# Routing of the first two chunks of a fused attention and expert kernel: small operands in a PSUM bank, comparisons over even then odd columns

## The chip, the cores and the metric

The program runs on one core of a Trainium2 chip. The metric is the device time of one execution in microseconds (us). Of the core's engines, TensorE (PE in the profile) multiplies matrices, VectorE (DVE) and ScalarE (ACT) work element by element on SBUF and PSUM, GpSimd (POOL) works on SBUF alone, and SyncE (SP) issues DMAs. PEld is PE's weight load. Each engine runs its own instructions in order and waits for the others by semaphores.

## What is computed

An attention with clusters as mask feeds a dense layer pair (MoE1), whose output is routed to one of eight experts for each token (MoE2). 2 x 768 = 1536 tokens of 512 values pass through all of it. The change touches the middle of the last function: norm, logits, arg-max, gate.

```python
def _moe_ref(x, w_in, w_out, s, b):            # MoE1: 512 -> 2048 -> 512
    h = x @ w_in
    r = np.maximum(h, 0.0)
    return (s * (r * r) + b) @ w_out

def _moe2_ref(x, expert_emb, tau, w1, w2):     # MoE2: 8 experts, 512 -> 1024 -> 512
    xn = x / (np.linalg.norm(x, axis=-1, keepdims=True) + 1e-06)
    en = expert_emb / (np.linalg.norm(expert_emb, axis=-1, keepdims=True) + 1e-06)
    logits = xn @ en.T / tau
    expert_idx = np.argmax(logits, axis=1)
    logits_shift = logits - logits.max(-1, keepdims=True)
    probs = np.exp(logits_shift)
    probs /= probs.sum(-1, keepdims=True) + 1e-09
    gate_w = probs[np.arange(N), expert_idx]
    for e in range(E):
        mask = expert_idx == e
        out[mask] = gate_w[mask, None] * (np.maximum(x[mask] @ w1[e], 0.0) @ w2[e])
```

## The kernel before

**Stages.** The span has three stages: attention (to about 290 us), MoE1 (to about 588 us), and the experts of MoE2. MoE1 takes the 1536 tokens in three chunks of 512. For a chunk it runs through 16 blocks f of the hidden width: `up(f)` multiplies the chunk by a weight block, `down(f-1)` multiplies the block before by its second weights into four PSUM banks y0 to y3. fp32 products are made from a high and a low part each, three matmuls for one. Per block that is 12 matmuls of up (L552, tile hp) and 12 of down (L560, tile y), each of 512 columns; such a block is called a round here.

**Who feeds a round.** ACT copies the weights' high part (L529, wh), POOL subtracts it for the low part (L531, two 128x512 `tensor_tensor` per round on SBUF). ACT and DVE then turn hp into the inputs of down: L607 (ACT, t), L608 (DVE, hp), L611 (ACT, gh), L612 (DVE, gl). In the last chunk POOL also makes the low part of three weight blocks of the first expert (L545, tile wu) and issues gathers by index (L824).

**Routing beside it.** When a chunk is done, `route` for it is a generator, and MoE1 takes one step of it per round of the next chunk (`next(stages)` in `moe1`), ordered behind that round's L611 and L612. So the routing of the first chunk (c = 0) runs in the rounds of the second, that of the second (c = 1) in the rounds of the third, and that of the third (`final`) after MoE1. Step by step: transposes (tp), projection (lt), logits (lg), arg-max as a one-hot (oh), rank of each token within its expert (rk, rank), `locate` (L721: DVE compares a row of 384 column numbers, `iotas`, with each token's rank, giving the 0/1 matrices ohr, in pieces of 256 and 128 columns), `collect` (L727: PE multiplies ohr with small values into tile si, and DVE adds si into `info`), then the norm by `root` (ACT, L82) and `norm_recip` (DVE, L86 to L91, on tile nr), the shifted logits (L760 to L762, on l), exp (ACT, L766), the gate (L767 to L775, on m, gt, gb, v) and a last `collect` of it. After the second locate, c = 1 also runs `pick` (which expert is worked early) and at its end `take`.

**Order and banks.** Within MoE1 the tile framework's scheduler orders each engine's instructions; there is no table. PSUM has eight banks, named here by tags: "a" stands for the bank pv, "b" for sm; y0 to y3 and M0, M1 (hp, in turns) are the other six. A tile on a tag waits until the last reader of the tile before it on that tag is done.

**The weight conversion.** During the first chunk DVE also turns w_in and w_out from 64-bit to 32-bit floats (`conv_steps`). Its clamp, L425, works in place in SBUF over even, then odd elements; the steps behind it write or read tile cv in PSUM (L430, L435, L437):

```python
s = t.rearrange("p a (w o) -> p o (a w)", o=2)
nc.vector.tensor_scalar(out=s.bitcast(F32), in0=s.bitcast(F32), scalar1=CLAMP_LO, scalar2=CLAMP_HI, op0=ALU.max, op1=ALU.min)
...
nc.vector.scalar_tensor_tensor(out=u[a], in0=r[a][:, :, 1], scalar=0xC0000000, in1=u[a], op0=ALU.bitwise_and, op1=ALU.bitwise_or)
nc.vector.scalar_tensor_tensor(out=t[:, a], in0=r[a][:, :, 0], scalar=29, in1=u[a], op0=ALU.logical_shift_right, op1=ALU.bitwise_or)
```

Of the kernel before, what the change touches and what calls it, by code (L numbers as in the profile page):

```python
# [9 lines left out]
F32 = mybir.dt.float32  # L10
# [6 lines left out]
ALU = mybir.AluOpType  # L17
AX = mybir.AxisListType
# [3 lines left out]
P = 128  # L22
# [17 lines left out]
E, F2 = 8, 1024  # L40
# [40 lines left out]
def root(nc, g):  # L81
    nc.scalar.activation(out=g(1), in_=g(0), func=AF.Sqrt)  # L82


def norm_recip(nc, g):
    nc.vector.tensor_scalar(out=g(4), in0=g(1), scalar1=1e-30, scalar2=None, op0=ALU.max)  # L86
    nc.vector.reciprocal(out=g(5), in_=g(4))
    nc.vector.tensor_tensor(out=g(6), in0=g(0), in1=g(5), op=ALU.mult)
    nc.vector.tensor_tensor(out=g(1), in0=g(6), in1=g(1), op=ALU.add)
    nc.vector.tensor_scalar(out=g(2), in0=g(1), scalar1=0.5, scalar2=1e-6, op0=ALU.mult, op1=ALU.add)  # L90
    nc.vector.reciprocal(out=g(3), in_=g(2))  # L91
# [289 lines left out]
class Moe:  # L381
# [262 lines left out]
    def route(self, c, ys, final):  # L644
        nc = self.nc
        n = len(ys)
        g0 = c * n
        fill = lambda i: final and self.fill(FILL[i])
        rp = self.sm
        bc = lambda a: a.to_broadcast([P, n, E])  # L650
# [10 lines left out]
        yt = []  # L661
        part = rp.tile([P, n, P], F32, name="part", tag="part", bufs=1)

        nr = rp.tile([P, n, 8], F32, name="nr", tag="nr")

        def square(i):
            sq = self.gp.tile([P, DM], F32, name="sq", tag="t", bufs=4)
# [17 lines left out]
        for i, t in enumerate(lt):  # L685
            copy(i, part[:, i * each:(i + 1) * each], t)
        yield
        lg = self.ps([P, n, E], "lg", "M0" if final else "b")
        for i in range(n):
            nc.tensor.matmul(lg[:, i], part[:, i], self.fold)  # L690
        fill(0)
        l = rp.tile([P, n, E], F32, name="l", tag="l")
        w = rp.tile([P, n, E], F32, name="w", tag="w")
        m = rp.tile([P, n, 4], F32, name="m", tag="m")
# [22 lines left out]
        ohr = [rp.tile([P, 3 * P], BF16, name="ohr", tag="ohr", bufs=4) for _ in range(n)]  # L717

        def locate(j0, j1):
            for i in range(n):  # L720
                nc.vector.tensor_scalar(out=ohr[i][:, j0 * P:j1 * P], in0=self.iotas[:, j0 * P:j1 * P], scalar1=self.rank[:, g0 + i:g0 + i + 1], scalar2=None, op0=ALU.is_equal)  # L721

        def collect(j0, j1, v0, v1, tag):
            si = self.ps([P, j1 - j0, v1 - v0, E], "si", tag)
            for j in range(j0, j1):
                for i in range(n):
                    nc.tensor.matmul(si[:, j - j0], ohr[i][:, j * P:(j + 1) * P], v[:, i, v0:v1], start=i == 0, stop=i == n - 1)  # L727
            self.accumulate(self.info[:, j0:j1, v0:v1], si, c)
            if final and v0 == 0:
                if j0 == 0:  # L730
                    self.where = [self.sm.tile([P, 3, E], dt, name=nm, tag=nm, bufs=1) for nm, dt in (("idx", U32), ("off", U32), ("gate", F32), ("dec", F32))]
                self.index(self.where[0][:, j0:j1], self.info[:, j0:j1])

        locate(0, 2)
        yield
        collect(0, 2, 0, 2, "b")
        fill(2)
        yield
        locate(2, 3)
        collect(2, 3, 0, 2, "a")  # L740
        fill(3)
# [14 lines left out]
            yield  # L756
        if not final:
            root(nc, lambda i: nr[:, :, i])
        norm_recip(nc, lambda i: nr[:, :, i])
        nc.vector.tensor_tensor(out=l, in0=l, in1=bc(nr[:, :, 3:4]), op=ALU.mult)  # L760
        nc.vector.tensor_reduce(out=m[:, :, 2:3], in_=l, axis=AX.X, op=ALU.max)
        nc.vector.tensor_tensor(out=l, in0=l, in1=bc(m[:, :, 2:3]), op=ALU.subtract)  # L762
        if final:
            fill(5)
        yield
        nc.scalar.activation(out=l, in_=l, func=AF.Exp)  # L766
        nc.vector.tensor_reduce(out=m[:, :, 3:4], in_=l, axis=AX.X, op=ALU.add)  # L767
        nc.vector.tensor_scalar(out=m[:, :, 3:4], in0=m[:, :, 3:4], scalar1=1e-9, scalar2=None, op0=ALU.add)
        gt = rp.tile([P, n, 4], F32, name="gt", tag="gt")
        gb = rp.tile([P, n, 3], BF16, name="gb", tag="gb")  # L770
        nc.vector.reciprocal(out=gt[:, :, 0:1], in_=m[:, :, 3:4])
        for z in range(3):
# [1 line left out]
            nc.vector.tensor_tensor(out=gt[:, :, z + 1:z + 2], in0=gt[:, :, z:z + 1], in1=gb[:, :, z:z + 1], op=ALU.subtract)  # L774
            nc.vector.tensor_tensor(out=v[:, :, 2 + z], in0=oh, in1=bc(gb[:, :, z:z + 1]), op=ALU.mult)  # L775
        yield
        collect(0, 3, 2, 5, "y0" if final else "b")
        if c == NT // TC - 2:
            self.take()
            yield  # L780
# [3 lines left out]
        if final:  # L784
            _, off, gate, a = self.where
            self.decode(off, gate, a, self.info, self.slot, self.ntok.rearrange("p (o e) -> p o e", o=1).to_broadcast([P, 3, E]))

    def pick(self):
        nc, sm = self.nc, self.sm
        ps = self.ps([P, E], "pk", "b")  # L790
        nc.tensor.matmul(ps, self.ones, self.cum)
        n, w, m0, m, keep, s = [sm.tile([P, E], F32, name=nm, tag=nm, bufs=1) for nm in ("pn", "pw", "pm0", "pm", "pk", "ps")]
        self.m0, self.m, self.keep, self.late, self.drop = m0, m, keep, s[:, 2:3], s[:, 3:4]
        nc.vector.tensor_copy(n, ps)
        nc.vector.tensor_reduce(out=s[:, 0:1], in_=n, axis=AX.X, op=ALU.max)
        nc.vector.scalar_tensor_tensor(out=w, in0=n, scalar=s[:, 0:1], in1=self.desc, op0=ALU.is_equal, op1=ALU.mult)
        nc.vector.tensor_reduce(out=s[:, 1:2], in_=w, axis=AX.X, op=ALU.max)
        nc.vector.tensor_scalar(out=m0, in0=w, scalar1=s[:, 1:2], scalar2=None, op0=ALU.is_equal)
        nc.vector.tensor_scalar(out=s[:, 2:3], in0=s[:, 0:1], scalar1=3.0 * P, scalar2=None, op0=ALU.is_ge)
        nc.vector.tensor_scalar(out=s[:, 3:4], in0=s[:, 0:1], scalar1=float(P), scalar2=None, op0=ALU.is_lt)  # L800
        nc.vector.tensor_scalar(out=s[:, 4:5], in0=s[:, 1:2], scalar1=-1.0, scalar2=float(E), op0=ALU.mult, op1=ALU.add)
        nc.vector.scalar_tensor_tensor(out=s[:, 5:6], in0=s[:, 0:1], scalar=float(P), in1=s[:, 2:3], op0=ALU.is_ge, op1=ALU.subtract)
        nc.vector.tensor_scalar(out=m, in0=m0, scalar1=s[:, 5:6], scalar2=None, op0=ALU.mult)
        nc.vector.tensor_scalar(out=keep, in0=m0, scalar1=s[:, 2:3], scalar2=None, op0=ALU.mult)
        nc.vector.tensor_scalar(out=keep, in0=keep, scalar1=float(2 * P - NT), scalar2=float(NT), op0=ALU.mult, op1=ALU.add)
        up = [self.xp.tile([P, 2, F2], F32, name="eup", tag=f"xt{i}") for i in range(2)]
        down = [self.xp.tile([P, 4, DM], F32, name="edn", tag="xt2")] + [self.raw.tile([P, 2, DM], F32, name="edn", tag="raw") for _ in range(2)]
        self.eup = [up[k // 2][:, k % 2] for k in range(KD)]
        self.edown = [down[0][:, f] if f < 4 else down[f // 2 - 1][:, f % 2] for f in range(NF2)]
        self.eload = []  # L810
        for tiles, src, each in ((up, self.w1, KD), (down, self.w2, NF2)):
            r0 = 0
            for i, t in enumerate(tiles):
                n = t.shape[1]
                r = sm.tile([P, 1], U32, name="wr", tag=f"wr{each}{i}", bufs=1)
                nc.vector.scalar_tensor_tensor(out=r, in0=s[:, 4:5], scalar=float(P), in1=self.iotap, op0=ALU.mult, op1=ALU.add)
                nc.vector.tensor_scalar(out=r, in0=r, scalar1=float(each // n), scalar2=float(r0 // n), op0=ALU.mult, op1=ALU.add)
                self.eload.append((t, src.rearrange("e (q r) w -> (e q) (r w)", r=n), r))
                r0 += n
# [34 lines left out]
    def fill(self, n):  # L854
        for _ in range(n):
            next(self.early, None)
# [335 lines left out]
```

## Time and profile before

| What | Value |
| --- | --- |
| Median of 3 runs | 823.32 us (821.75 to 825.11) |
| Profiled execution, its own time | 824.21 us |
| Its span in the profile | 822.3 us |
| PE busy | 769.7 us (94%) |
| DVE busy | 526.9 us (64%) |
| ACT busy | 421.6 us (51%) |
| POOL busy | 347.5 us (42%) |

The engines' busy times are sums over the whole span. Times in the rows are counted from the span's start. In a row of the timeline the first number is the start, the second how long the row lasted, from the start of its first instruction to the end of its last; a bracket at the end holds the idle time of the engine before it and who ended it. An instruction that is held up inside its engine is not idle there: it shows as a long one.

### The profile page before, as it was taken

What the parts mean: (1) busy time and instruction counts of PE and PEld (TensorE: products, weight loads), DVE (VectorE), ACT (ScalarE), POOL (GpSimd) and SP (SyncE); (2) the same over time, 40 slices, a digit from 0 to 9 for tenths busy, and PEclk for the clock granted to TensorE, in tenths of its full rate; (3) what the DMA queues carried; (4) which work ended last, traced back from release to release, by engine and by line L of the source; (5) the groups of instructions that cost most, each with busy time, mean ns of one, the idle gap of its engine ahead of it and who ended that gap; (6) DMA issues with size and microseconds to landing.
All of it is one profiled execution on the core that took longest, in us unless ns stands there. A gap on an engine that the chain in (4) does not pass through costs nothing. (4 is left out here: it accounts for less than half of the span.)

```text
span 822.3 us, 12229 instructions
## 1 busy us (share of the span) xinstructions
PE 769.7 (94%) x4191; PEld 580.2 (71%) x4193; DVE 526.9 (64%) x1087; ACT 421.6 (51%) x841; POOL 347.5 (42%) x277
## 2 busy tenths in 40 slices
PE   7699999898998889999999999997999999999994
PEld 3456555454554458888778787775879998989883
DVE  5769789695895779994353642648446635756650
ACT  5355465454653665646445554444346645756651
POOL 2067766575674655435434443445032202220000
PEclk9799999998998999999999999989999999999998
DMA  5155423334232205611000042254131844876600
GB/s 147 49 139 175 124 72 92 111 91 119 73 76 63 60 22 170 184 55 52 1 1 1 7 147 86 94 191 142 65 103 58 272 141 157 236 259 228 211 17 23
DMA packets 75470, 88.73 MB, mean 108 GB/s; under 512 B 7445, under 2 KB 58549, under 8 KB 75008
## 3 DMA queue, kind: packets, MB, share of 16 engines
q1 hardware_dynamic: 68704, 69.67, 27.9%
q0 software_dynamic: 4000, 13.90, 5.3%
q10 hardware_dynamic: 2688, 4.19, 1.7%
q8 instruction: 40, 0.66, 0.3%
q14 instruction: 38, 0.31, 0.1%
HBM read 70.57 MB, written 7.34 MB: 95 GB/s over the span
## 5 line engine op out<-in xcount | busy, mean ns | idle before, releaser
L531 POOL TENSOR_TENSOR wl<-w,wh 128x512 fp32r<-128x512 f32 x96 | 123.1, 1307 | 131.5 <-ACT wh L529 128.9
L249 ACT ACTIVATE pt<-S 128x384 f32<-128x384 f32 x192 | 91.6, 490 | 123.1 <-PE S L248 121.0
L224 DVE TENSOR_REDUCE mx<-M 128x1 f32<-128x384 f32 x192 | 101.8, 551 | 54.8 <-PE M L223 52.8
L260 POOL TENSOR_TENSOR acc<-acc,pt 128x768 f32<-128x768 f32 x61 | 106.1, 1740 | 6.5 <-ACT pt L249 4.1
L552 PE MATMUL hp<-x,wh 128*128 128x512 f32 x384 | 107.2, 400 | 0.3 <-ACT wh L529 0.3
L552 PE MATMUL hp<-x,spare 128*128 128x256 f32 x732 | 96.1, 284 | 2.0 <-PEq L984 1.7
L552 PEld LDWEIGHTS hp<-x,spare 128*128 128x128 f32 x732 | 92.7, 190 | 6.9 <-issue 4.1
L560 PE MATMUL y<-wd,gg 128*128 128x512 f32 x360 | 93.2, 395 | 0.0
L608 DVE SCALAR_TENSOR_TENSOR hp<-hp,sb,t 128x512 f32<-128x512 f32 x48 | 36.3, 757 | 78.8 <-ACT t L607 78.8
L247 PE MATMUL S<-qa,ka 97*128 97x384 f32 x192 | 72.5, 377 | 13.2 <-DMA qa<-mrs 11.5
L552 PEld LDWEIGHTS hp<-x,wh 128*128 128x128 f32 x384 | 71.9, 191 | 15.5 <-ACT wh L529 0.9
L223 PE MATMUL M<-ka,qa 80*128 80x384 f32 x192 | 79.0, 412 | 3.6 <-DVE mx L224 2.3
L268 PE MATMUL pv<-pt,vn 128*64 128x385 f32 x384 | 78.8, 534 | 0.0
L560 PE MATMUL y<-wh,gh 128*128 128x512 f32 x192 | 75.6, 394 | 1.7 <-ACT gh L611 1.7
L560 PE MATMUL y<-wl,gh 128*128 128x512 f32 x192 | 75.3, 392 | 0.0
L545 DVE TENSOR_TENSOR wd<-w,wd 128x512 fp32r<-128x512 f32 x64 | 43.3, 686 | 44.4 <-ACT wd L544 41.0
L560 PEld LDWEIGHTS y<-wd,gg 128*128 128x128 f32 x360 | 63.7, 189 | 10.1 <-DVE gg L1081 0.2
L1033 POOL DMA_INDIRECT row<-rows,idx x24 | 28.0, 1166 | 95.7 <-PE tp L1045 50.8
L248 PE MATMUL S<-qb,kb 128*128 128x384 f32 x192 | 66.7, 347 | 0.0
L607 ACT ACTIVATE t<-hp 128x512 f32<-128x512 f32 x48 | 28.7, 598 | 73.9 <-PE hp L552 73.9
L223 PEld LDWEIGHTS M<-ka,qa 80*128 80x128 f32 x192 | 37.1, 193 | 39.2 <-issue 8.2
L560 PE MATMUL y<-wh,gl 128*128 128x512 f32 x192 | 59.4, 391 | 0.0
(269 smaller groups left out, 1371.8 us busy)
## 6 DMA issues: line engine op xcount, KB each, us to landing
w<-in_moe_w_dram SPq DMA_DIRECT2D x128, 256.0 KB
raw<-in_moe_w_in_dram SPq DMA_DIRECT2D x12, 512.0 KB
raw<-in_moe_w_out_dram SPq DMA_DIRECT2D x12, 512.0 KB
qn<-in_q_dram SPq DMA_DIRECT2D x16, 192.0 KB
kn<-in_k_dram SPq DMA_DIRECT2D x16, 192.0 KB
vn<-in_v_dram SPq DMA_DIRECT2D x16, 192.0 KB
ka<-kb SPq DMA_DIRECT2D x16, 192.0 KB
qa<-qb SPq DMA_DIRECT2D x16, 192.0 KB
```

Of the source, the lines that this page charges most:

```text
L223: nc.tensor.matmul(pp, qa[i][0:80, r * P:(r + 1) * P], ka[i][0:80, c * HS:(c + 1) * HS])
L224: nc.vector.tensor_reduce(out=mxt[j % 2][:, r, c:c + 1], in_=pp, axis=AX.X, op=ALU.max)
L247: nc.tensor.matmul(pp, ka[i][0:97, t * P:(t + 1) * P], qa[i][0:97, w], start=True, stop=False)
L248: nc.tensor.matmul(pp, kb[i][:, t * P:(t + 1) * P], qb[i][:, w], start=False, stop=True)
L249: exps.setdefault((j, t), []).append(nc.scalar.activation(out=p[:, c, 0:HS], in_=pp, func=AF.Exp, scale=0.125).ins)
L260: eng.tensor_tensor(out=acc[j][-1], in0=acc[j][-1], in1=p[:, :, 0:HS], op=ALU.add)
L268: together(tc, [lambda c=c: nc.tensor.matmul(pv_t[j][c * 64:c * 64 + 64, :], io_t["v", j][:, t, :], p[:, c, :], start=t == 0, stop=t == NR ...
L531: eng.tensor_tensor(out=wl[:, a], in0=w[:, a], in1=wh[:, a].bitcast(F32), op=ALU.subtract)
L545: eng.tensor_tensor(out=t[:, 1], in0=w[:, a], in1=t[:, 0].bitcast(F32), op=ALU.subtract)
L552: self.nc.tensor.matmul(hp, a[:, k * P:(k + 1) * P], b(k), start=n == 0, stop=n == 3 * KD - 1)
L560: self.nc.tensor.matmul(y[i], (gl if n == 2 else gh)[:, s], wl if n == 1 else wh, start=first and n == 0, stop=last and n == 2)
L608: nc.vector.scalar_tensor_tensor(out=hp, in0=hp, scalar=sb[:, 0:1], in1=t, op0=ALU.mult, op1=ALU.mult)
```

## The change

In the routing of all three chunks one PSUM tile `rt` takes the place of `lg`, on the same tag ("b", in the final chunk M0), and lives until the gate is done. It holds the logits (`lg`), the intermediate results of `norm_recip` and the row maximum (`nb`, eight numbers per token tile) and the gate's residues (`gt`), which were SBUF tiles; of `nr` two columns stay in SBUF, the squared norm and its root. In the first two chunks the tiles `si` and `pk`, which were on "b", go to "a", and `locate` compares the even columns first and then the odd ones, in one instruction with a pattern of 2 x 128 (or 2 x 64) in steps of two.

```diff
-        nr = rp.tile([P, n, 8], F32, name="nr", tag="nr")
+        nr = rp.tile([P, n, 2], F32, name="nr", tag="nr")
...
-        lg = self.ps([P, n, E], "lg", "M0" if final else "b")
+        rt = self.ps([P, 3, n, 32], "rt", "M0" if final else "b")
+        lg, nb, gt = rt[:, 0, :, 0:E], rt[:, 1, :, 0:8], rt[:, 2, :, 0:4]
...
         def locate(j0, j1):
             for i in range(n):
-                nc.vector.tensor_scalar(out=ohr[i][:, j0 * P:j1 * P], in0=self.iotas[:, j0 * P:j1 * P], scalar1=self.rank[:, g0 + i:g0 + i + 1], scalar2=None, op0=ALU.is_equal)
+                o, s = [t[:, j0 * P:j1 * P] for t in (ohr[i], self.iotas)]
+                if not final:
+                    o, s = [t.rearrange("p (w o) -> p o w", o=2) for t in (o, s)]
+                nc.vector.tensor_scalar(out=o, in0=s, scalar1=self.rank[:, g0 + i:g0 + i + 1], scalar2=None, op0=ALU.is_equal)
...
-        collect(0, 2, 0, 2, "b")
+        collect(0, 2, 0, 2, "b" if final else "a")
...
-        norm_recip(nc, lambda i: nr[:, :, i])
-        nc.vector.tensor_tensor(out=l, in0=l, in1=bc(nr[:, :, 3:4]), op=ALU.mult)
-        nc.vector.tensor_reduce(out=m[:, :, 2:3], in_=l, axis=AX.X, op=ALU.max)
-        nc.vector.tensor_tensor(out=l, in0=l, in1=bc(m[:, :, 2:3]), op=ALU.subtract)
+        norm_recip(nc, lambda i: (nr if i < 2 else nb)[:, :, i])
+        nc.vector.tensor_tensor(out=l, in0=l, in1=bc(nb[:, :, 3:4]), op=ALU.mult)
+        nc.vector.tensor_reduce(out=nb[:, :, 7:8], in_=l, axis=AX.X, op=ALU.max)
+        nc.vector.tensor_tensor(out=l, in0=l, in1=bc(nb[:, :, 7:8]), op=ALU.subtract)
...
-        gt = rp.tile([P, n, 4], F32, name="gt", tag="gt")
...
-        collect(0, 3, 2, 5, "y0" if final else "b")
+        collect(0, 3, 2, 5, "y0" if final else "a")
...
-        ps = self.ps([P, E], "pk", "b")
+        ps = self.ps([P, E], "pk", "a")
```

DVE's norm step in the routing of the second chunk, before:

```order
L86 TENSOR_SCALAR nr<-nr 128x4
L87 RECIPROCAL nr<-nr 128x4
L88 TENSOR_TENSOR nr<-nr 128x4
L89 TENSOR_TENSOR nr<-nr 128x4
L90 TENSOR_SCALAR nr<-nr 128x4
L91 RECIPROCAL nr<-nr 128x4
L760 TENSOR_TENSOR l<-l,nr 128x32
L761 TENSOR_REDUCE m<-l 128x4
L762 TENSOR_TENSOR l<-l,m 128x32
```

The same step after, where rt is the PSUM bank and nr, l are in SBUF:

```order
L86 TENSOR_SCALAR rt<-nr 128x4
L87 RECIPROCAL rt<-rt 128x4
L88 TENSOR_TENSOR rt<-nr,rt 128x4
L89 TENSOR_TENSOR nr<-rt,nr 128x4
L90 TENSOR_SCALAR rt<-nr 128x4
L91 RECIPROCAL rt<-rt 128x4
L764 TENSOR_TENSOR l<-l,rt 128x32
L765 TENSOR_REDUCE rt<-l 128x4
L766 TENSOR_TENSOR l<-l,rt 128x32
```

Nothing moved on DVE: the same nine instructions stand in the same place, and each `tensor_tensor` that had two SBUF inputs has one now.

DVE's gate step behind it, after (before, rt reads gt and the lines are L767, L768, L771 and L773 to L775; the last three come three times):

```order
L771 TENSOR_REDUCE m<-l 128x4
L772 TENSOR_SCALAR m<-m 128x4
L774 RECIPROCAL rt<-m 128x4
L776 CAST gb<-rt 128x4
L777 TENSOR_TENSOR rt<-rt,gb 128x4
L778 TENSOR_TENSOR vals<-oh,gb 128x4x8
```

L772, which reads and writes SBUF, and L778, with two SBUF inputs (oh and gb), are as they were.

PE around the second locate of the second chunk's routing, before (hp is the round's up, si the collect, pk of `pick`; a bracket says which engines an instruction waits for):

```order
L552 MATMUL hp<-x,wh 128x512 x2
L727 LDWEIGHTS ohr [waits DVE_49]
L727 MATMUL si<-vals,ohr 128x16 [waits PE_49]
L552 MATMUL hp<-x,wh 128x512
L727 LDWEIGHTS ohr [waits DVE_49]
L727 MATMUL si<-vals,ohr 128x16
L552 MATMUL hp<-x,wh 128x512
L727 LDWEIGHTS ohr [waits DVE_49]
...
L727 MATMUL si<-vals,ohr 128x16
L552 MATMUL hp<-x,wl 128x512 [waits Pool_49]
L791 LDWEIGHTS onesb [waits DVE_49]
L791 MATMUL pk<-cum,onesb 128x8 [waits PE_49]
```

The same place after:

```order
L552 MATMUL hp<-x,wh 128x512 x3
L731 LDWEIGHTS ohr [waits DVE_49]
L731 MATMUL si<-vals,ohr 128x16 [waits PE_49]
L731 LDWEIGHTS ohr [waits DVE_49]
L731 MATMUL si<-vals,ohr 128x16
L552 MATMUL hp<-x,wh 128x512
L731 LDWEIGHTS ohr [waits DVE_49]
L731 MATMUL si<-vals,ohr 128x16
L552 MATMUL hp<-x,wl 128x512 [waits Pool_49]
L731 LDWEIGHTS ohr [waits DVE_49]
L731 MATMUL si<-vals,ohr 128x16
...
L794 MATMUL pk<-cum,onesb 128x8 [waits DVE_49]
```

One matmul of hp moved ahead of the first si, two stand between the last si and pk, and pk waits for DVE, which reads si on the same bank.

## Rows read from the trace of the kernel before

**Rows 1.** Who PE waited for, 300 to 640 us: total, times, longest.

```profile
PE si L727 <- DVE vals L775: 4.5, 2, 3.6
PE si L727 <- DVE ohr L721: 2.4, 3, 1.0
PE y L560 <- ACT gh L611: 1.7, 1, 1.7
```

**Rows 2.** Stretches of 10 us: PE, PEld, DVE, ACT, POOL busy, granted clock, DMA.

```profile
530.00:540.00 10.00, 7.61 (x27) 5.24 (x27) 7.84 (x31) 2.42 (x4) 4.77 (x5) 0.78 0.32 105
550.00:560.00 10.00, 10.00 (x45) 8.27 (x45) 5.42 (x5) 6.05 (x10) 8.79 (x8) 1.00 0.48 154
570.00:580.00 10.00, 8.51 (x41) 6.92 (x41) 8.49 (x34) 3.02 (x5) 1.72 (x2) 0.83 0.27 79
```

**Rows 3.** Timeline of PE, gate of c = 1: start, length, instruction, idle before.

```profile
560.25 1.07 PE L552 MATMUL hp<-x,wh 128*128 128x512 f32 x4
...
564.86 0.50 PE L560 MATMUL y<-wh,gh 128*128 128x512 f32 x1 [1.73 <-ACT gh L611]
...
571.49 0.45 PE L727 MATMUL si<-vals,ohr 128*128 128x24 bf16 x12 [3.62 <-DVE vals L775]
...
578.95 1.07 PE L552 MATMUL hp<-x,wh 128*128 128x512 f32 x4
```

**Rows 4.** Timeline of PE, gate of c = 0.

```profile
459.85 1.07 PE L552 MATMUL hp<-x,wh 128*128 128x512 f32 x4
...
466.28 0.46 PE L727 MATMUL si<-vals,ohr 128*128 128x24 bf16 x12 [0.84 <-DVE vals L775]
...
472.19 1.07 PE L552 MATMUL hp<-x,wh 128*128 128x512 f32 x4
```

**Rows 5.** Timeline of DVE: norm step of c = 0, then norm and gate of c = 1.

```profile
456.04 0.17 DVE L88 TENSOR_TENSOR nr<-nr 128x4 f32<-128x4 f32 x1
...
556.48 5.64 DVE L88 TENSOR_TENSOR nr<-nr 128x4 f32<-128x4 f32 x1
...
563.33 0.75 DVE L608 SCALAR_TENSOR_TENSOR hp<-hp,sb,t 128x512 f32<-128x512 f32 x1
...
567.02 1.24 DVE L773 CAST gb<-gt 128x4 bf16<-128x4 f32 x1
```

**Rows 6.** Timeline of POOL in the same stretch.

```profile
556.03 1.00 POOL L824 DMA_INDIRECT edn<-in_moe_w_dram,wr  x1 [0.16 <-issue]
557.06 5.02 POOL L531 TENSOR_TENSOR wl<-w,wh 128x512 fp32r<-128x512 f32 x4
566.95 1.29 POOL L545 TENSOR_TENSOR wu<-w,wu 128x512 fp32r<-128x512 f32 x1 [4.87 <-ACT wu L544]
```

**Rows 7.** Timeline of PE: second locate of c = 0, then of c = 1.

```profile
437.49 0.61 PE L552 MATMUL hp<-x,wh 128*128 128x512 f32 x2
...
443.52 1.07 PE L552 MATMUL hp<-x,wh 128*128 128x512 f32 x4
...
532.08 0.61 PE L552 MATMUL hp<-x,wh 128*128 128x512 f32 x2
...
543.93 1.07 PE L552 MATMUL hp<-x,wh 128*128 128x512 f32 x4
```

**Rows 8.** Timeline of DVE and POOL: second locate of c = 1.

```profile
532.37 3.84 DVE L721 TENSOR_SCALAR ohr<-iotas,rank 128x128 bf16<-128x128 f16 x4
...
533.50 2.51 POOL L531 TENSOR_TENSOR wl<-w,wh 128x512 fp32r<-128x512 f32 x2
```

**Rows 9.** Timeline of DVE and POOL: weight conversion in the first chunk (cv in PSUM).

```profile
307.51 0.68 DVE L437 SCALAR_TENSOR_TENSOR w<-raw,cv 128x512 uint32<-128x512 uint32 x1
308.11 0.69 DVE L435 SCALAR_TENSOR_TENSOR cv<-raw,cv 128x512 uint32<-128x512 uint32 x1
308.71 1.74 DVE L425 TENSOR_SCALAR w<-w 128x1024 f32<-128x1024 f32 x1
...
307.34 4.26 POOL L531 TENSOR_TENSOR wl<-w,wh 128x512 fp32r<-128x512 f32 x3
```

**Rows 10.** Who PE waited for, from 585 us to the end of the span.

```profile
PE hp L552 <- PEq L984: 1.7, 4, 0.4
```

## The prediction

> **What bounds the kernel now.** Read first the share of busy time: PE is busy for 94% of the span, so a change is worth what it takes from PE's idle time, or from PE's clock. Then the list of PE's waits, narrowed to MoE1 [rows 1]: between 300 and 640 us PE waited for only three things, and all three are routing. 4.5 us went to the gate's values (two waits), 2.4 us to the comparisons of locate (three waits), 1.7 us to gh. The table of stretches shows the second price [rows 2]: beside an undisturbed stretch at clock 1.00 stand two at 0.78 and 0.83, those that hold the waits. The granted clock has two levels, 2.4 and 1.2 GHz, and PE spent part of these stretches at the lower one, after standing idle. So a wait is priced by how much longer its rounds took, not by the idle time alone.
>
> Three places follow, named A, B and C.
>
> **C**, the gate of c = 1. Two rounds, from 560.25 to 578.95, took 18.70 us [rows 3]. The same two rounds in the routing of c = 0 run from 459.85 to 472.19, 12.34 us, with one wait of 0.84 in them [rows 4], so 11.50 without it. C costs 18.70 - 11.50 = 7.20 us, of which 1.73 + 3.62 = 5.35 is idle time and the rest the clock.
>
> **A** is that wait of 0.84 in c = 0 [rows 4]; no clock was lost there.
>
> **B**, the second locate of c = 1: the round took 543.93 - 532.08 = 11.85 us, its counterpart in c = 0 443.52 - 437.49 = 6.03 [rows 7]. B costs 5.8 us, less some 0.1 for the pk matmul that c = 0 has not.
>
> **Why C waits.** L88 is a product of four numbers per partition. It took 0.17 us for c = 0 and 5.64 for c = 1 [rows 5]. It started at 556.48, while POOL ran an indirect DMA, and ended with POOL's train of four subtractions, 557.06 + 5.02 = 562.08 [rows 6]. DVE stood in it, and all else on DVE stood behind it: L608 came at 563.33, gh behind that (PE's 1.73), and exp and the gate behind gh (PE's 3.62). The cast in the gate took 1.24 beside POOL's subtraction of 1.29 that had started just before it [rows 5, 6]. So some DVE instructions are held while POOL works.
>
> **Which instructions are held.** Rows 9 separate the kinds. POOL ran three subtractions from 307.34 on. Under them L437 and L435, with one input in SBUF and one in PSUM, took 0.68 and 0.69. L425, a tensor_scalar from SBUF to SBUF, took 1.74. So one SBUF input beside a PSUM operand goes free; SBUF to SBUF with a scalar is held, and so are two SBUF inputs (L88). The Trainium skill says the same in "SBUF — State Buffer", § Who interferes with whom: a VectorE instruction in a two-port mode or with two SBUF inputs and a GpSimd instruction exclude each other for the whole instruction. By that rule L88 would have lost one subtraction, about 1.3 us, not four; the row is longer, and I go by the row.
>
> **The change, part by part.**
>
> *Norm step in PSUM.* L88, L89 and the two products on l now have one SBUF input each, the others read or write PSUM. By rows 9 none is held: the step costs nine short instructions, and L88 is back at about c = 0's 0.17. That takes 5.64 - 0.17 = 5.5 us out of DVE ahead of L608, so gh is there when down begins (1.73 gone), and exp and the gate start earlier by as much.
>
> *Gate step.* Cast and residue (L776, L777) are free now. Two kinds stay as they were: L772, SBUF to SBUF, and three L778 with two SBUF inputs. Each can lose a turn of POOL, 1.26 us (5.02 / 4 [rows 6]). c = 0 is the case with L88 not held and a gate step that still meets POOL, and there PE waited 0.84. So what stays of C is between 0 (no turn lost) and 0.84 (as c = 0, since the free casts are offset by held L778). I take 0.4, the middle, and no clock, since A lost none. C gains 7.2 - 0.4 = 6.8. For A the bounds are a gain of 0.84 and of 0; I take 0.4 too. For both together the likely gain is 7.2, between 6.4 and 8.0.
>
> *Even, then odd columns.* The trace has no 16-bit comparison of this form, so it is bounded by neighbours. L425 is the nearest: a tensor_scalar from SBUF to SBUF whose code also takes even, then odd elements, and it was held (1.74 [rows 9]). The cast, whose output is 16 bits wide in steps of three, was held as well (1.24 [rows 5]). So neither the steps nor the width frees an instruction, and I expect the four comparisons at B to be held as before: they took 3.84 us while POOL had one subtraction running and two more to 536.01 [rows 8]. Gain 0. The other end is that the form goes free, which gains B's 5.7; that is the first rival. The comparison's own length changes little: L425's 1.74 with a turn of 1.26 in it leaves some 0.5 us for 1024 columns, so 128 columns stay under 0.1.
>
> The Trainium skill bears on just this part. "VectorE: DVE Perf Modes", § What auto-detection actually checks, says that pairs of 16-bit elements need a step of one, and that the two-port mode asks for one SBUF source, an SBUF destination and an even outermost dimension. A 2 x 64 pattern keeps the second and loses the first, so by the page it is still a two-port instruction, and is held. By the page the sum keeps B as it is; no run here shows that form yet.
>
> *PE's order at B.* The order after has one more hp matmul ahead of the first si and two behind the last one ahead of pk, which now also waits for DVE to read si. DVE's read of si and the matmuls between cover it; I put it at 0, between -0.3 and +0.3.
>
> *Banks.* All of si on one bank: the first and the last collect write a round (about 5.4 to 6 us) after the bank's last reader, so nothing waits. rt keeps its bank for several rounds, and no other tile of the loop uses that tag meanwhile. In the final chunk rt keeps M0 until the gate is done; the first expert's hp on M0 stands behind the gate's collect on PE anyway. Cost 0; the early expert's matmuls cover it, and if that cover were short PE would show a wait there, where it has none [rows 10]. The final chunk has no POOL subtraction, so nothing is gained there.
>
> **What comes after.** A gain in MoE1 reaches the end only if nothing later is fixed in time. From 585 us on PE waits for no engine and no DMA, 1.7 us of branches apart [rows 10]; so the later work moves up whole.
>
> **Sum.** 6.8 (C) + 0.4 (A) + 0 (B) = 7.2 us. Against the profiled execution, 824.21 us for a span of 822.3: 817.0. That execution lies 0.9 us above the median of the runs, 823.32, and the forecast goes by the median: 823.3 - 7.2 = 816.1 us.
>
> **Rivals.**
>
> 1. *The strided comparison goes free too.* For it: the pattern is used only where POOL works, and no row has this very form under POOL. Against it: L425 and the cast. The result is B's 5.7 on top: 823.3 - 7.2 - 5.7 = 810.4.
>
> 2. *The hold moves on.* L88's long hold began under the indirect DMA ahead of POOL's train. If L772 or the first L778, both still exposed, meets a train and loses all of it as L88 did, the gate is late instead of the norm. Then gh comes in time (1.73 saved) but PE waits before si as it did (3.62), with the clock. Against it: the cast lost only one turn. C then gains about 2, with nothing at A: 821.3.
>
> 3. *Slower: the strided comparisons take a fourth turn of POOL.* It needs that L88's hold is not one of two SBUF inputs but of the indirect DMA, and holds any DVE instruction, so that C gains nothing. Then a comparison at B that is a little longer misses the gap in which the fourth now follows the third, and POOL's next subtraction goes first: 1.26 more for DVE and PE, at half the clock for the matmuls behind it, which makes it about 2.5. Result 825.8. The point from which it decides is the presence of a further POOL subtraction when the third comparison ends; rows 8 show POOL done at 536.01 before the comparisons end at 536.21, which speaks against it, as L437 and L435 do.
>
> **How the numbers follow.** Forecast 816.1: 0.58. Rival 1: 0.20. Rival 2: 0.13. Rival 3: 0.09. The range reaches from 809.5, to hold rival 1 with a gain of 0.9 for the bounds of A and C, to 819.8, the forecast with A and C at their lower end (0.8), the wait at B longer by 0.3 and some 2.5 us for the spread of the runs (821.75 to 825.11). Left out are rivals 2 and 3, about 0.2. The bound of 0.5% is about what a measurement of this kernel tells from no change, 4.1 us, or 819.2 and 827.4. Faster: the forecast but for its upper edge, and rival 1, 0.76. Same: that edge, rival 2, most of rival 3, 0.20. Slower: the upper part of rival 3, 0.04.
>
> **What would show it right or wrong.** Right: L88 at about 0.2 for c = 1 though POOL runs beside it; no wait of PE for gh; a wait for the gate's values under 0.9 in both chunks; the clock at 1.00 where C was; the strided L725 for four comparisons still near 3.8 at B, with PE waiting some 2.5 and the clock down once. Wrong: the comparisons at B near 1 us in all (rival 1); L772 or L778 above 3 us (rival 2); L88 long again, with more than three of POOL's turns inside the comparisons (rival 3).

## The result and the profile after

| What | Before | After |
| --- | --- | --- |
| Median of 20 runs each, taken side by side | 824.8 us (818.25 to 826.92) | 815.21 us (810.85 to 820.64) |
| Profiled execution, its own time | 824.21 us | 812.13 us |
| Its span | 822.3 us | 810.3 us |
| Mean granted clock of the span | 0.967 | 0.971 |
| PE busy | 769.7 us | 764.7 us |

The ratio after to before is 0.9893, with a 95% interval of 0.9876 to 0.9909: the change saves 8.8 us of 824.8, between 7.5 and 10.2. The forecast was a gain of 7.2 and a time of 816.1 us.

In the changed kernel the lines have moved by three or four: L721 (locate) is now L725, L727 (collect) L731, L772 to L775 (gate) L774 and L776 to L778. Norm and gate values appear under the name of the bank, `rt`.

Read first who PE waited for between 300 and 640 us, the view of [rows 1]; columns: total, times, longest.

```profile
PE si L731 <- DVE ohr L725: 2.5, 3, 1.0
```

Of three lines one is left. The waits for the gate's values (4.5 us) and for gh (1.7 us) are gone, the waits for the comparisons at B are as they were. Beyond 575 us PE waits for no engine and no DMA here either; the branches' 1.7 us of [rows 10] are the only line.

The stretches of [rows 2] lie up to 10 us earlier now (columns: PE, PEld, DVE, ACT, POOL busy, granted clock, DMA share, GB/s). B is in the first, C in the second and third.

```profile
530.00:540.00 10.00, 9.29 (x29) 6.69 (x29) 5.31 (x29) 3.16 (x7) 4.09 (x4) 0.66 0.45 152
550.00:560.00 10.00, 10.00 (x46) 8.29 (x45) 6.75 (x23) 6.97 (x10) 9.82 (x9) 1.00 0.69 241
560.00:570.00 10.00, 9.91 (x55) 8.04 (x54) 8.20 (x30) 3.14 (x6) 2.03 (x2) 1.00 0.27 85
```

The clock now falls at B only. Where C stood, with a clock of 0.83, it is 1.00 and PE is busy but for 0.09 us.

The timeline of DVE shows why (start, length, instruction): norm step and gate of c = 1, to be read against [rows 5].

```profile
551.62 0.17 DVE L88 TENSOR_TENSOR rt<-nr,rt 128x4 f32<-128x4 f32 x1
...
553.53 0.76 DVE L608 SCALAR_TENSOR_TENSOR hp<-hp,sb,t 128x512 f32<-128x512 f32 x1 [0.46 <-ACT t L607]
...
556.81 0.49 DVE L772 TENSOR_SCALAR m<-m 128x4 f32<-128x4 f32 x1
...
557.56 0.17 DVE L776 CAST gb<-rt 128x4 bf16<-128x4 f32 x1
...
557.84 0.73 DVE L778 TENSOR_TENSOR vals<-oh,gb 128x32 bf16<-128x32 bf16 x1
...
558.77 1.05 DVE L778 TENSOR_TENSOR vals<-oh,gb 128x32 bf16<-128x32 bf16 x1
...
560.00 1.06 DVE L778 TENSOR_TENSOR vals<-oh,gb 128x32 bf16<-128x32 bf16 x1
```

And POOL in the same stretch, beside [rows 6].

```profile
551.20 1.00 POOL L827 DMA_INDIRECT edn<-in_moe_w_dram,wr  x1 [0.16 <-issue]
552.23 5.04 POOL L531 TENSOR_TENSOR wl<-w,wh 128x512 fp32r<-128x512 f32 x4
557.24 1.29 POOL L545 TENSOR_TENSOR wu<-w,wu 128x512 fp32r<-128x512 f32 x1
558.49 2.52 POOL L531 TENSOR_TENSOR wl<-w,wh 128x512 fp32r<-128x512 f32 x2
```

A turn is the time of one subtraction on POOL, about 1.26 us; a train is several of them without a gap. POOL does what it did before: the indirect DMA, then a train of four subtractions. L88 starts under the same indirect DMA as before and takes 0.17 us in place of 5.64. What is not in PSUM is still held: L772 ends at 557.30, with the fourth subtraction (557.27), and each of the three L778 loses a turn or the rest of one. Here POOL's next subtractions follow on the train without a gap, to 561.01, and L772 was let in ahead of them. None of it reaches PE. On PE's timeline the gate's collect (its row of before is in [rows 3]) shows no wait:

```profile
555.42 1.07 PE L552 MATMUL hp<-x,wh 128*128 128x512 f32 x4
...
561.12 0.45 PE L731 MATMUL si<-vals,ohr 128*128 128x24 bf16 x12
...
566.96 1.07 PE L552 MATMUL hp<-x,wh 128*128 128x512 f32 x4
```

**Where the time went.** MoE1 is cut out of the two spans from PE's first hp matmul in it to the first transpose of the early expert (tpe). Of before, then of after:

```profile
298.08 1.20 PE L552 MATMUL hp<-x,wh 128*128 128x512 f32 x4 [0.28 <-ACT wh L529]
...
584.39 0.63 PE L863 MATMUL tpe<-ident,row 128*128 128x128 f32 x4
```

```profile
294.05 1.19 PE L552 MATMUL hp<-x,wh 128*128 128x512 f32 x4 [0.54 <-ACT wh L529]
...
572.40 0.63 PE L866 MATMUL tpe<-ident,row 128*128 128x128 f32 x4
```

That is 286.31 and 278.35 us, 7.96 less. The rounds of the three places add up to it. Where A and B begin and end in after (those of before are in [rows 4] and [rows 7]), and the comparisons at B:

```profile
455.82 1.07 PE L552 MATMUL hp<-x,wh 128*128 128x512 f32 x4
...
467.13 1.07 PE L552 MATMUL hp<-x,wh 128*128 128x512 f32 x4
...
527.01 0.84 PE L552 MATMUL hp<-x,wh 128*128 128x512 f32 x3
...
539.09 1.08 PE L552 MATMUL hp<-x,wh 128*128 128x512 f32 x4
```

```profile
527.30 3.92 DVE L725 TENSOR_SCALAR ohr<-iotas,rank 128x128 bf16<-128x128 f16 x4
```

| Place | Before | After | Difference |
| --- | --- | --- | --- |
| A, two rounds (459.85 to 472.19; 455.82 to 467.13) | 12.34 | 11.31 | -1.03 |
| B, one round (532.08 to 543.93; 527.01 to 539.09) | 11.85 | 12.08 | +0.23 |
| C, two rounds (560.25 to 578.95; 555.42 to 566.96) | 18.70 | 11.54 | -7.16 |
| Sum | | | -7.96 |

The spans differ by 12.0. The other 4.03 us lie ahead of MoE1, which began at 298.08 and at 294.05, in the attention, which the change does not touch: over the eleven profiles of this study MoE1 begins anywhere between 293.54 and 298.69. So a difference of two spans says little here, and the length of MoE1 is used below beside the ratios.

### The profile page after: what moved, and what is told of

It is laid out like the page before. It is cut to its first block, busy times and chain, and to the rows that moved or that the text cites. A ratio compares the mean times of both kernels' runs of the same rounds, so it can differ in the third digit from the quotient of the medians.

```text
span 810.3 us, 12231 instructions
## 1 busy us (share of the span) xinstructions
PE 764.7 (94%) x4193; PEld 578.5 (71%) x4193; DVE 521.3 (64%) x1087; ACT 422.0 (52%) x841; POOL 347.6 (43%) x277
## 5 line engine op out<-in xcount | busy, mean ns | idle before, releaser
L608 DVE SCALAR_TENSOR_TENSOR hp<-hp,sb,t 128x512 f32<-128x512 f32 x48 | 36.3, 757 | 75.3 <-ACT t L607 75.2
L247 PE MATMUL S<-qa,ka 97*128 97x384 f32 x192 | 72.7, 379 | 12.7 <-DMA qa<-mrs 11.0
L560 PEld LDWEIGHTS y<-wd,gg 128*128 128x128 f32 x360 | 63.7, 189 | 10.1 <-DVE gg L1084 0.2
```

The source lines that it names most:

```text
L247: nc.tensor.matmul(pp, ka[i][0:97, t * P:(t + 1) * P], qa[i][0:97, w], start=True, stop=False)
L560: self.nc.tensor.matmul(y[i], (gl if n == 2 else gh)[:, s], wl if n == 1 else wh, start=first and n == 0, stop=last and n == 2)
L608: nc.vector.scalar_tensor_tensor(out=hp, in0=hp, scalar=sb[:, 0:1], in1=t, op0=ALU.mult, op1=ALU.mult)
```

## The experiments

The theory is the prediction's. A DVE instruction with two SBUF inputs, or one from SBUF to SBUF with a scalar, is held while POOL subtracts; one PSUM operand frees it, and even-then-odd columns do not. The rivals: the strided form is what gains; the hold moves on; L88's long hold comes of the indirect DMA and holds any instruction. In the table MoE1 is cut as above.

| Kernel | Median, us | Its before, us | Ratio, 95% | MoE1, us |
| --- | --- | --- | --- | --- |
| e1, strided comparison alone | 824.33 | 822.56 | 1.002 (0.9991 to 1.005) | 286.13 |
| e2, PSUM operands alone | 812.96 | 822.56 | 0.988 (0.9845 to 0.9916) | 278.24 |
| e3, norm step alone in PSUM | 812.54 | 822.56 | 0.9877 (0.9832 to 0.9922) | 277.58 |
| e4, e2 and column numbers in PSUM | 805.75 | 822.56 | 0.9796 (0.9757 to 0.9835) | 272.69 |
| e5, e2 and wu a round earlier | 810.1 | 821.34 | 0.9854 (0.981 to 0.9897) | 272.31 |
| e6, L88's reciprocal alone in PSUM | 818.61 | 821.34 | 0.9959 (0.9928 to 0.9989) | 285.59 |
| e7, gate alone in PSUM | 819.28 | 821.34 | 0.9976 (0.9944 to 1.0007) | 283.20 |
| e8, last two gathers in one round | 822.21 | 821.34 | 1.0014 (0.9982 to 1.0046) | 286.52 |
| e9, all gathers in the pick's round | 815.27 | 823.22 | 0.9902 (0.9869 to 0.9935) | 280.45 |

e1 to e4, e5 to e8 and e9 each ran beside their own runs of the kernel before. A gain "by the ratio" below is worked out from the ratio and its interval; MoE1 comes from one execution each.

**e1: the strided comparison alone.** The kernel before, with this hunk of the change only:

```diff
-                nc.vector.tensor_scalar(out=ohr[i][:, j0 * P:j1 * P], in0=self.iotas[:, j0 * P:j1 * P], ...)
+                o, s = [t[:, j0 * P:j1 * P] for t in (ohr[i], self.iotas)]
+                if not final:
+                    o, s = [t.rearrange("p (w o) -> p o w", o=2) for t in (o, s)]
+                nc.vector.tensor_scalar(out=o, in0=s, ...)
```

> The kernel before with the even, then odd comparisons in the first two chunks' locate and nothing else; nr, gt and the banks as before. Theory (the strided form is held by POOL as the plain one is, and the gain is the norm step's): 0, between -1 and +1 us against before; the four comparisons at the second locate of c = 1 stay near 3.8 us, L88 of c = 1 stays at several us, PE's three waits stay. Rival (the strided form is part of the 9.6 us): -2 to -6 us, and the four comparisons fall to about 1 us.

The time is that of before, and so is MoE1 (286.13 against 286.31). The timeline of DVE, the comparisons at B and L88 of c = 1:

```profile
530.19 3.92 DVE L724 TENSOR_SCALAR ohr<-iotas,rank 128x128 bf16<-128x128 f16 x4
...
554.15 5.64 DVE L88 TENSOR_TENSOR nr<-nr 128x4 f32<-128x4 f32 x1
```

And PE's waits, 300 to 640 us, are the three of [rows 1] again, with the same lengths: 4.5, 2.4 and 1.7 us.

So the strided form is held as the plain one is: 3.92 us for four against 3.84 in [rows 8]. Without POOL beside them four strided comparisons of 128 columns take 0.89 us (c = 0 of the changed kernel) and plain ones 0.74 (there before). The form also brought the new order of PE at B, three hp matmuls ahead of the first si, which is therefore worth nothing either.

**e2: the PSUM operands alone.** The changed kernel with the plain comparison, that is, the change without e1's hunk.

> The changed kernel with the plain comparisons put back, so the PSUM bank and the tags alone. Theory: the whole gain, -8 us (7.2 for the stretch of the gate of c = 1 and 0.84 for c = 0), between -6.5 and -10; PE's waits for gh and for the gate's values are gone. Rival (the strided form is part of the gain): -4 to -6.

PE's waits are down to the one that after has, for the comparisons at B (2.4 us in three parts).

The time is that of after: ratio 0.988 beside 0.9893 (a gain of 9.9 us, 6.9 to 12.7), MoE1 278.24 beside 278.35. The whole gain is that of the PSUM operands.

**e3: the norm step alone in PSUM.** As e2, with the gate's values back in SBUF:

```diff
-        lg, nb, gt = rt[:, 0, :, 0:E], rt[:, 1, :, 0:8], rt[:, 2, :, 0:4]
+        lg, nb = rt[:, 0, :, 0:E], rt[:, 1, :, 0:8]
...
+        gt = rp.tile([P, n, 4], F32, name="gt", tag="gt")
```

> The PSUM bank with the logits and the norm's intermediate results (nb), but the gate's residues gt in SBUF as before; plain comparisons. Theory by the rows of after, where PE did not wait at all at the gates: L88 is the cause and is free, -7 us, between -5 and -8; the cast and the residue are held for a turn of POOL each again, so PE waits up to 1 us for the gate's values in each chunk. Rival (the gate step carries as much): -3 or less.

The gate is held again, and PE waits for it once; first its cast and residue on DVE's timeline for c = 1, then PE's waits:

```profile
556.33 1.00 DVE L774 CAST gb<-gt 128x4 bf16<-128x4 f32 x1
557.37 1.20 DVE L775 TENSOR_TENSOR gt<-gt,gb 128x4 f32<-128x4 f32 x1
```

```profile
PE si L728 <- DVE ohr L722: 2.4, 3, 1.0
PE si L728 <- DVE vals L776: 0.9, 1, 0.9
```

Yet MoE1 is no longer than in e2 (277.58). The 0.9 of the wait is there: C's two rounds took 12.31 us, where e2's took 11.56. But the round at B took 10.59 us in this execution and 11.97 in e2's, which outweighs it. By the ratio the gain is 10.1 us (6.4 to 13.8), by MoE1 8.7, both above the 5 to 8 that were expected; the gate of c = 0, where a wait was expected too, has none. The ratios (0.9877 and 0.988) can't tell the two kernels apart: once the norm step is free, the trace has the gate's share as that one wait of 0.9 us, and the times don't show it.

**e7: the gate alone in PSUM.** The counterpart, again from e2: the norm step's values in an SBUF tile, the gate's in PSUM.

```diff
+        nb = rp.tile([P, n, 8], F32, name="nb", tag="nb")
...
-        lg, nb, gt = rt[:, 0, :, 0:E], rt[:, 1, :, 0:8], rt[:, 2, :, 0:4]
+        lg, gt = rt[:, 0, :, 0:E], rt[:, 2, :, 0:4]
```

> As e2, but the norm's intermediate results are in SBUF; the gate's residues are in PSUM. Theory: L88 of c = 1 is held as before, so PE still waits 1.7 us for gh; of the wait for the gate's values the turns of POOL that the casts lost may go: 0 to -2 us against before. Rival (the gate's casts carry half of the gain): -4 or more.

L88 is held as before, and PE waits for gh and the gate behind it:

```profile
PE si L729 <- DVE vals L776: 3.2, 2, 2.9
PE si L729 <- DVE ohr L723: 2.3, 3, 1.0
PE y L560 <- ACT gh L611: 1.7, 1, 1.7
```

The wait for the values falls by 1.3 us (4.5 to 3.2) and MoE1 by 3.1; by the ratio the gain is 2.0 us, not clear of noise (-0.6 to 4.6). By the traces, then, the gate's operands in PSUM are worth something while the gate is late, and under 1 us once the norm step is free.

**e6: one operand of L88 in PSUM.** The reciprocal that L87 writes goes to PSUM, the other intermediate results of `norm_recip` stay in SBUF, so that L88 has one SBUF input and L89, the next product of four numbers, has two. The row maximum and the gate are in PSUM as in after; the diff is against e2.

```diff
-        nr = rp.tile([P, n, 2], F32, name="nr", tag="nr")
+        nr = rp.tile([P, n, 8], F32, name="nr", tag="nr")
...
-        norm_recip(nc, lambda i: (nr if i < 2 else nb)[:, :, i])
+        norm_recip(nc, lambda i: (nb if i == 5 else nr)[:, :, i])
-        nc.vector.tensor_tensor(out=l, in0=l, in1=bc(nb[:, :, 3:4]), op=ALU.mult)
+        nc.vector.tensor_tensor(out=l, in0=l, in1=bc(nr[:, :, 3:4]), op=ALU.mult)
```

> As e2, but of the norm's intermediate results only the reciprocal that L88 reads is in PSUM; the others are in SBUF, so L88 has one SBUF input and L89, right behind it, two. Theory (what is held is any product or sum of two SBUF inputs that is issued while POOL works there): L89 of c = 1 is held in L88's place, 5 us or more, and hardly anything of the gain is left: 0 to -3 us against before. Rival (L88 alone is held, for what it is or where it starts): L89 takes 0.2 us and the gain is that of e2.

DVE's timeline of c = 1, and POOL's:

```profile
553.93 0.16 DVE L88 TENSOR_TENSOR nr<-nr,rt 128x4 f32<-128x4 f32 x1
554.13 5.44 DVE L89 TENSOR_TENSOR nr<-nr 128x4 f32<-128x4 f32 x1
```

```profile
553.48 1.00 POOL L824 DMA_INDIRECT edn<-in_moe_w_dram,wr  x1 [0.16 <-issue]
554.51 5.02 POOL L531 TENSOR_TENSOR wl<-w,wh 128x512 fp32r<-128x512 f32 x4
```

This is the cleanest pair of rows of the study. L88 and L89 are both products of four numbers, one behind the other, under the same indirect DMA. The one with a PSUM input takes 0.16 us; the one with two SBUF inputs stands until the train ends at 559.53. So it is the operands, not the place, that decide. The third rival's premise, that the indirect DMA holds any DVE instruction, falls. MoE1 gains only 0.7 us by it (by the ratio 3.4, 0.9 to 5.9), and that is A's, whose two rounds take 11.31 us; C's two take 18.89 (557.71 to 576.60), no less than before. A hold that is taken from one instruction goes to the next that is exposed, so all of the step has to move.

**e4: the comparisons' input in PSUM.** B is untouched by the change. Here the third piece of the column numbers is copied into the last quarter of the routing's bank, and the second locate compares from there.

```diff
-        rt = self.ps([P, 3, n, 32], "rt", "M0" if final else "b")
+        rt = self.ps([P, 4, n, 32], "rt", "M0" if final else "b")
+        col = rt[:, 3].rearrange("p n w -> p (n w)")
...
+                s = col if j0 == 2 and not final else self.iotas[:, j0 * P:j1 * P]
...
+        if not final:
+            nc.vector.tensor_copy(col, self.iotas[:, 2 * P:3 * P])
```

> The bank as in the changed kernel, plain comparisons, and the column numbers of the second locate (128 of 384) copied by DVE into the last quarter of the same bank right after the first locate; the second locate of the first two chunks compares from there, so its input is in PSUM. Theory (an SBUF-to-SBUF comparison is held for one turn of POOL each, and that is all of the cost at the second locate of c = 1): the four comparisons take about 0.9 us at c = 1, PE does not wait for them, its clock stays up, and the 5.7 us of that round go: -13 to -14 us against before. Rival (something else holds PE there, such as POOL's extra subtraction for wu, which PE waits for by wl): -8 us as without it, with the wait under another name.

DVE and POOL at B:

```profile
526.78 1.12 DVE L724 TENSOR_SCALAR ohr<-rt,rank 128x128 bf16<-128x128 f32 x4
```

```profile
526.67 1.30 POOL L545 TENSOR_TENSOR wu<-w,wu 128x512 fp32r<-128x512 f32 x1 [2.00 <-ACT wu L544]
527.93 2.52 POOL L531 TENSOR_TENSOR wl<-w,wh 128x512 fp32r<-128x512 f32 x2
```

Four comparisons in 1.12 us under POOL's subtractions, where they took 3.84 in [rows 8]; the round at B takes 6.46 us (526.49 to 532.95), and PE has no wait left between 300 and 640 us. At 805.75 us, 2% below its before, this version beats both kernels: by the ratio it gains 16.8 us (13.6 to 20.0), by MoE1 13.6, where 13 to 14 were expected. What the even-then-odd form did not do, the PSUM input does.

**e5: POOL out of the way at B.** The other remedy: e2 with the subtraction of wu at B a round earlier.

```diff
-PRE0 = (9, 11, 13)
+PRE0 = (8, 11, 13)
```

> The PSUM bank with plain comparisons (as e2), and the first of POOL's three subtractions for the first expert (wu) moved one block earlier, from f = 9 to f = 8, out of the round of the second locate of c = 1. Theory (that subtraction is what lets the comparisons of c = 1 meet POOL, since c = 0 has none there and took 0.74 us): the four comparisons take about 0.7 us, PE does not wait, and the round's 5.7 us go as in e4: -13 to -17 us against before. Rival (POOL's subtractions for wl come early enough by themselves): -8 to -10, as e2.

DVE at B, then POOL, whose next subtraction now starts after the comparisons:

```profile
531.87 0.73 DVE L722 TENSOR_SCALAR ohr<-iotas,rank 128x128 bf16<-128x128 f16 x4
```

```profile
532.97 2.55 POOL L531 TENSOR_TENSOR wl<-w,wh 128x512 fp32r<-128x512 f32 x2 [3.17 <-ACT wh L529]
```

The round takes 6.16 us (531.58 to 537.74) and MoE1 272.31, 5.9 below e2 and 14.0 below before. By the ratio the gain is 12.0 us (8.5 to 15.6), less than the 13 to 17 expected and not clear of the rival's 8 to 10; it is the round that decides between the two. It is the collision with POOL that B pays for; by MoE1, moving either party away gains the same.

**e8: no indirect DMA during the norm step.** Left over is the length of L88's hold, the whole train, where casts and comparisons lost one turn each. In e8 the kernel before issues its last two gathers in one round, so that none runs while the norm step does:

```diff
                     self.eweights()
+                    if len(self.eload) == 1:
+                        self.eweights()
```

> The kernel before with the last two of the five early weight gathers issued by POOL in the same round, so that no indirect DMA runs when the norm step of c = 1 starts; POOL then runs six subtractions in a row there. Theory A (a product of two SBUF inputs loses one turn of POOL when it meets a train, and L88 lost four because it was issued during the indirect DMA): L88 takes 1.3 us or less, and the time is 4 to 7 us less than before. Theory B (it is held to the end of a train whenever it is issued): L88 takes 5 us or more, and the time is as before, within 2 us.

DVE's norm step of c = 1, and POOL:

```profile
551.35 6.12 DVE L86 TENSOR_SCALAR nr<-nr 128x4 f32<-128x4 f32 x1 [0.77 <-ACT nr L82]
```

```profile
548.92 0.99 POOL L826 DMA_INDIRECT edn<-in_moe_w_dram,wr  x1 [0.30 <-issue]
549.93 7.50 POOL L531 TENSOR_TENSOR wl<-w,wh 128x512 fp32r<-128x512 f32 x6
```

Now L86, from SBUF to SBUF with a scalar, is the first to meet the train, 1.4 us into it, and it stands to the train's end at 557.43. So a long hold does not need an indirect DMA that is running when the instruction starts: theory B's outcome, though on L86 and not on L88. The time is that of before. PE's wait for the gate's values fell to 2.0 us at C (3.62 in [rows 3]), yet C's two rounds took 18.80 us (555.95 to 574.75; before 18.70), at a granted clock of 0.82 in place of 0.91: idle time alone would have misjudged them.

**e9: no indirect DMA ahead of the train.** All five gathers in the round of the pick, where the last two stood in later rounds before:

```diff
-                    self.eweights()
+                    while self.eload:
+                        self.eweights()
```

> The kernel before, with all five gathers of the early expert's weight rows issued in the round of the pick, so that no indirect DMA stands on GpSimd's queue ahead of the train of weight subtractions beside the norm step of the second chunk. The arithmetic is unchanged. Theory one (a train of weight subtractions keeps a comparing or multiplying VectorE instruction out to its end only where an indirect DMA stands directly ahead of it): the held instruction of the norm step of the second chunk takes 1.3 us or less, one turn of the train, PE's wait for vals falls from 4.5 us to 2 us or less, and the time is 4 to 7 us below the kernel before, 816 to 819 us. Theory two (a train of ready subtractions keeps it out whatever stands ahead of it): the instruction takes 3 us or more and ends with the train, PE's wait for vals stays at 2.5 us or more, and the time is within 2.5 us of the kernel before. The gathers ahead may put back the subtractions beside the second locate of the second chunk; that would show there, as another duration of the four comparisons than 3.84 us.

DVE's norm step of c = 1, and POOL:

```profile
546.34 1.22 DVE L86 TENSOR_SCALAR nr<-nr 128x4 f32<-128x4 f32 x1 [0.77 <-ACT nr L82]
...
547.81 0.99 DVE L88 TENSOR_TENSOR nr<-nr 128x4 f32<-128x4 f32 x1
548.84 1.22 DVE L89 TENSOR_TENSOR nr<-nr 128x4 f32<-128x4 f32 x1
550.09 1.21 DVE L90 TENSOR_SCALAR nr<-nr 128x4 f32<-128x4 f32 x1
...
551.55 1.02 DVE L761 TENSOR_TENSOR l<-l,nr 128x32 f32<-128x32 f32 x1
...
552.82 0.99 DVE L763 TENSOR_TENSOR l<-l,m 128x32 f32<-128x32 f32 x1
```

```profile
543.77 2.53 POOL L545 TENSOR_TENSOR wu<-w,wu 128x512 fp32r<-128x512 f32 x2 [4.37 <-ACT wu L544]
546.27 7.49 POOL L531 TENSOR_TENSOR wl<-w,wh 128x512 fp32r<-128x512 f32 x6
```

Again six subtractions without a gap, and nobody is kept out to the end: each instruction loses one turn. As theory one had it, the long hold goes with an indirect DMA directly ahead of the train. Theory one's other number fell: PE's wait for vals stays at 4.4 us in all, 3.6 at the gate of c = 1. All six rows above were held, the four of the norm and the two products on l, and six single turns cost 5.6 us above the unheld lengths, as much as the one long hold did (5.64 less 0.17); the gate lost three more (1.24, 1.18, 1.22). So the gain by the ratio, 8.1 us (5.4 to 10.8), overlaps the 4 to 7 that were given for it, but most of it is not the one that was meant. In this version POOL makes wu only at 543.77, after a wait of 4.37 us for ACT, so the comparisons at B are free of it: they took 0.74 us and the round 6.15 (528.00 to 534.15), 5.7 less than before. C's two rounds (552.27 to 569.11, 16.84) give 1.9, and the round ahead of them, in which PE has a new wait of 1.5 us for wl, takes back 1.8 (7.24 for 5.44). That leaves 5.8, against the 5.9 by which MoE1 is shorter.

## Why the prediction was right

**C, its mechanism.** Right. L88 0.17 under the same train, gh in time, no wait at the gate, clock 1.00. e2 puts the whole gain on the PSUM operands, e3 nearly all of it on the norm step, and e6 puts the hold on the second SBUF input, on two neighbouring rows. Why L88 lost four turns and not one the prediction left open; e8 and e9 narrow it down and do not settle it.

**C and A, their sizes.** Both a little too small: 6.8 + 0.4 were put in, 7.16 + 1.03 came. The step that failed is the reading of c = 0 as the case in which only the gate still meets POOL; its wait of 0.84 was put down to the gate's held instructions and carried over to C as the upper bound of what stays. But c = 0 had two held instructions in its norm step as well, the products on l. DVE's timeline of before:

```profile
456.87 1.08 DVE L760 TENSOR_TENSOR l<-l,nr 128x32 f32<-128x32 f32 x1
...
458.20 1.00 DVE L762 TENSOR_TENSOR l<-l,m 128x32 f32<-128x32 f32 x1
```

In after L764 and L766 take 0.19 each, which takes 1.7 us (1.08 + 1.00 less twice 0.19) out of DVE. L608 behind them then waits 0.46 us for ACT, so the gate starts 1.16 us earlier in PE's round: it began 2.32 us into it before (462.17 less 459.85) and begins 1.16 into it in after (456.98 less 455.82). That is more than the 0.84 by which it was late. e3 shows that this is enough: there the gate of c = 0 is still in SBUF and a cast and a residue of it lose a turn each (1.26 and 1.20), and PE's collect has no wait:

```profile
461.54 0.46 PE L728 MATMUL si<-vals,ohr 128*128 128x24 bf16 x12
```

So nothing stays at A or C, though turns are lost in the gate of after as said (0.49, 0.73, 1.05 and 1.06 for c = 1): they fit into the slack that the norm step gives back. The lower of the two bounds for what stays was the true one at both places. At A the gain of 1.03 lies above even the 0.84 that was its upper bound: that bound was the idle time, while the round with the wait took 6.75 us before (459.85 to 466.60) and 5.75 in after (455.82 to 461.57). The prediction's own rule, to price a wait by its rounds, was not applied there.

**B.** Right: 0 was put in, the comparisons took 3.92 (3.84), PE waited 2.5 (2.4), and the round took 12.08 (11.85). The 0.23 is within the spread of that round between executions with the same wait (10.59 in e3, 11.97 in e2). The neighbour that the bound rested on, L425, even-then-odd and held, was the right one. The side estimate that 128 columns stay under 0.1 us was low, as the 0.89 us for four show, but under POOL the turns set the time. By the Trainium skill, "VectorE: DVE Perf Modes", § What auto-detection actually checks, the strided pattern stays a two-port instruction; the 3.92 agrees.

**Rivals.** The first (strided form free) falls with e1. The second (the hold moves on to L772 or L778) falls in its size, but not by much of a margin: L772 did meet the train behind the indirect DMA, for its last half microsecond (557.27 less 556.81), and e6 and e8 show whole trains lost by whichever exposed instruction came first. By these rows a gate that started some 4 us sooner would have met most of that train; this was not tried. The third needed L88 to be held whatever its operands; e6 and after exclude it, and POOL still takes three turns at B.

**What comes after, the order, the banks.** Right at 0: from MoE1 on the work moved up whole, e1 shows PE's new order at B to be worth nothing, and no wait for a bank appeared.

**The total.** 7.96 in MoE1 against 7.2, and 8.8 (7.5 to 10.2) by the runs, so the gain that was put in lies just below the interval. That the time came within 0.9 us of 816.1 is in part luck: the kernel before took 824.8 us beside the changed one, 1.5 more than the 823.32 that the forecast started from, and this hides part of the shortfall.

## What to carry to other kernels

A DVE instruction on four numbers can cost 5 to 6 us while GpSimd works through a train of `tensor_tensor`, if both its inputs are in SBUF (L88, L89) or if it goes from SBUF to SBUF with a scalar (L86 in e8); look for short instructions with long rows, and read what GpSimd did at that time. Where PSUM has a bank to spare, put one operand of every exposed instruction of the step there, and not of the first alone (e6), for the hold goes on to the next; for a comparison against constants, a copy of the constants in PSUM does it (e4), a change of access pattern does not (e1). Price a wait of PE by its rounds, not by its idle time (A, e8), and compare the stretch that a change touches rather than two spans.

## What the runs showed of the hardware

- **A hold has two lengths.** In five kernels (before, e1, e6, e7 and e8) a DVE instruction on four numbers per partition, L86, L88 or L89, was kept out to the end of a train of four or six GpSimd subtractions (5.44 to 6.12 us), and each of these trains followed directly on an indirect DMA. Where a train began otherwise (the six of e9, the two beside the norm step of c = 0 in before, the three at B), each held instruction lost one turn (0.99 to 1.22 in e9). The Trainium skill, "SBUF — State Buffer", § Who interferes with whom, has the one that issues second blocked for the whole of the other's instruction; the second kind agrees with it, the first does not, and there the measured rows decide. What the indirect DMA does to the train was not found out, and it may be something that only goes with it: e9 has two more subtractions directly ahead of its six, and in after L772 was let in behind the fourth subtraction of such a train although POOL went on without a gap.
- **The clock's price varies.** The same 2.3 to 2.5 us of waits at B stand in eight of the kernels. The round took 11.65 to 12.08 us in seven of them, at a granted clock of 0.71 or 0.72, and 10.59 in e3, at 0.84; an undisturbed one takes 6.0 to 6.5 at 1.00. So the part that is not the wait, 2 to 3.5 us, is time at the lower clock, and a forecast that removes or adds such a wait carries this spread.
